# Unread matmuls ahead of the first spectra, u as the moving operand of the gate sums, and unsummed pairs of Q rows, in a gated mix of two long convolutions

## The chip, the cores and the metric

The kernel runs on one core of one Trainium2 chip. Its time is the device time in microseconds (us), the median of several runs. TensorE is called PE in what follows, its weight loads PEld, VectorE DVE, ScalarE ACT, GpSimd POOL, and the queue that starts most transfers SP.

## The reference

All inputs are bf16. The sequence has 2048 steps, the width is 448, and there are 256 complex modes for every channel. The two branches are long causal convolutions over the sequence, mixed by a gate that is computed from the same input x.

```
g = sigmoid(sum over channels of x * gate_w)              # one value for each step

# branch A: a state-space layer
K[d, l] = Re sum_n C[d,n] * exp(dt[d] * A[d,n] * l) * dt[d] * B[d,n]      # l = 0 .. 2047
a = causal_conv(x, K) + x * Dskip

# branch B: a gated convolution with a given kernel
kv = (k convolved with 4 taps of shift_k) * v
b = x * (causal_conv(kv, ssm_k) + kv * ssm_D)

out = g * a + (1 - g) * b
```

The reference computes the convolutions with transforms of length 4096.

## The kernel before

**Stages.** The 448 channels are cut into four groups of 112 (a group of 32 partitions each), and these into NQG = 4 quarters H of NC = 28. A convolution goes through a transform that is factored into matmuls. `spread` multiplies every column with a small matrix (Wc, or WcK for the kernel K) into the PSUM tile ps_c, which ACT casts to a spectrum tile zs (zsK for the kernel's). `transform` then multiplies it with W2 (s_W in the profile), four groups of eight matmuls of 112 columns, each through a PSUM tile ps and an ACT cast back to zs. `swapped` makes a copy zsS of a spectrum with its halves exchanged, by two transfers on SP. `products` multiplies spectra on DVE. `stage_a` (matrix R, the tile sa_R; PSUM tile ps_a; ACT casts into U) and `stage_b` (matrix G, the tile sb_G; PSUM tile ps_b) are the way back. Every quarter of each branch takes these stages. The spectra of branch B come from raw rows of ssm_k (skraw) and from kv, those of branch A from x (the tile uu) and from K.

**The kernel K.** K is made in NBLK = 8 blocks of 14 columns in `KGen.block`, so that 2048 steps arise from a product of two smaller tables of powers. DVE builds a table TQ (kg_TQ, NQ = 21 rows) and a table TP (kg_TP, 32 rows) of complex powers by doubling. `mult` makes the four real products of some rows with the power of one exponent (into P4, kg_P in the profile), and `add` sums pairs of them to new rows. Row groups of TQ arise for the exponents 4, 2, 256, 1 and 512. The rows for exponent 1 are not used for any further power. Then 224 small matmuls, `lhsT=TQ[:, :, c, m]` and 32 moving columns of TP, sum over the modes in the PSUM tile pk, in four column groups of the array (`tile_position=(0, 32 * g)`). ACT casts pk to kg_S, and `gather` sums the right rows of it with a table of zeros and ones (ga_sel), which `Consts.rows` and `Consts.gather` have set up at the start, into kg_KT.

The powers of one exponent, exp and sine for each mode, are made for two blocks at a time in `Tables.levels` (tiles ks_mag, ks_ph, ET): DVE makes phases, ACT the exponentials and sines. The two functions lie in different tables of ACT, and a change from one to the other costs a table load.

**The gate sums.** x * gate_w is summed over channels on PE. For every l of 112, a matmul has `uu[:, :, l]` (128 partitions, 64 columns that lie 112 elements apart) as weights and `gwt[:, l, :]` (32 columns) as the moving operand, and all 112 add up in one PSUM tile, ps_gate:

```
for l in range(112):
    nc.tensor.matmul(pg[0:64, 0:32], lhsT=uu[:, :, l], rhs=gwt[:, l, :], start=(l == 0), stop=(l == 111))
```

A copy (gx) and a transpose spread the sums over the partitions, and tanh gives the gate (gt, and from it gb and og).

**The start.** k arrives in sixteen transfers. `kvt` products on DVE, matmuls with an identity (PSUM tile ps_v) and ACT casts convolve it with the four taps. Meanwhile the modes are transposed (ps_m), and the matrices W2, G, R and so on are made of phases on DVE and sines on ACT.

**The end.** The last spectrum, K of the last quarter, is transformed in two halves by `transform_half`; `stage_a_half` and `stage_b` follow, then `epilogue_A` and the stores of the result.

**The order.** Nothing is issued when the code calls it. `Order` records all the calls of all engines (6452 here) in a list, and `Order.issue` issues them in the order of the string ORDER, a list of call numbers that was written beforehand; each engine runs its own instructions strictly in that order. This is why nearly all instructions have line 146, the line of `issue`, in the profile. They are told apart by their tiles.

Of the kernel before, what the change touches and what calls it, by code (L numbers as in the profile page):

```python
# [31 lines left out]
NQ = 21  # L32
# [9 lines left out]
    "600 25 576 30 164 1 190 525 24 36 188 196 162 189 175 177 23 34 186 191-192 187 176 193 526 534 26 31 552 173 "  # L42
    "171 580 174 536 581 0 32 160 593 537 2 166 172 528 33 73 535 598 21 179 17 35 540 11 10 14 3 22 28 75 16 6 182 "
    "178 13 18 12 29 15 7 19 198 184 9 38 591 8 5 20 4 37 181 74 65 180 183 39 76 201 27 161 550 197 577 168 200 167 "
    "41 542 163 544 589 169 165 194 79 590 40 582 170 541 195 42 599 583 52 199 185 202 586 592 69 584 587 585 588 "
    "100 46-47 203 50 72 51 553 44 595 204 594 551 43 538 48 45 110 66 49 557 68 77 101-108 90 53 78 55 554 71 56 539 "
    "150 54 596 63 556 111-118 67 109 62 597 70 527 91-98 555 80 61 64 119 529 140 531 151-158 99 530 234-241 602 545 "
    "130 141-148 159 242 215-222 543 532 120 149 225-232 548 205-212 223 233 213 267 214 549 243-250 224 252-259 547 "
    "251 81-88 533 546 260 121-128 89 319-326 129 262 268-283 261 327 131-138 284 264 263 285-300 139 266 302-317 265 "
    "301 575 516 499 318 493 1104 366 574 469 346-353 486 365 1106 1103 354 367 1105 471 502 470 364 474 473 472 468 "  # L50
    "481 370-385 490 573 477 570 498 562 578 507 567 489 513 561 482 560 494 815-830 483 512 478 579 479 495 484 487 "
    "491 496 488 480 492 485 503 603-616 521 497 522 504 1121 524 523 500 508 505 514 1108 617-630 501 509 517 1110 "
    "506 1109 631-644 510 518 1111 511 645-658 1119 558 1112 1122 1113 659-672 568 1117 673-686 572 559 1115 475 2483 "
    "687-700 566 515 563 1118 571 565 701-714 1124 831 1120 386 60 57-58 1126 798-813 1114 59 715 476 421-428 564 "
    "1123 716 814 1116 1107 1125 429 1510-1517 1846 717 1127 569 1476-1491 1518 2514 328-335 2498 1492 2515 781-796 "
    "519 1847 2497 2489 1848 718 404-419 2488 1129 520 720 1131 2487 719 1128 2491 2486 2492 2485 1133 797 1130 1132 "
    "420 1459-1474 1136 601 336 772-779 1135 1475 337-344 2490 1134 387-402 345 1137 2484 1849 832-839 780 1138 403 "
    "355-362 1850 840 1331-1362 1851 363 1267-1330 2499 1852 369 430-437 448-455 439-446 1853 368 1139-1202 1854 456 "
    "2518 2500 447 2519 1857 1203-1266 1856 2516 1855 438 946-953 2517 2509 1363 1860 1859 2510 1862 2511 1858 "
    "457-464 2520 755-770 2512 954 2521 1382-1421 2506 2502 465 1864 1493-1508 2505 2503 1422 1844 467 937-944 2507 "  # L60
    "1364-1380 1842 2504 1843 1381 1841 1509 1432-1439 2508 2538 2513 2494 721-736 2537 771 2493 2539 466 2495 "
    "738-753 737 754 2496 1639-1646 2533 2532 2540 2501 858-873 2558 2529 945 2528 2557 1861 1845 2522 901-908 2559 "
    "874 1863 1865 909 928-935 1867 1869 1647 2560 892-899 1871 936 2561 910-917 1866 900 919-926 918 1870 955-962 "
    "927 841-856 1868 2530 1872 1455 1648-1655 963 2563 1456 857 875-890 2531 2523 2565 1656 964-971 2524 2568 891 "
    "1873 1440 1038-1101 1874 2534 2525 1875 972 1441-1446 2535 1876 2552 1457 2069-2100 1877-1940 2544 2553-2554 "
    "2546 2005-2068 2549 1102 2545 2555 2550 1941-2004 2536 1458 2548 1447 2543 2541 2556 2551 3326 2547 1448-1453 "
    "2526 1613-1628 2542 2570-2571 2101 3328 3963 3327 2527 2573 1666-1673 1454 2562 1629 1657-1664 1423-1430 1674 "
    "2575 1579-1594 2564 1665 2566 1519-1534 2567 1595 3329 973-1036 3999 3966 3990 3965 3989 3970 3998 3330 3968 "
    "2569 3967 2197-2212 3972 1037 3964 1431 3971 2120-2159 2572 2213 1570-1577 6189 2160 1596-1611 1578 3331 1535 "
    "2102-2118 2574 1536-1551 3969 3333 2119 2577 1612 1630-1637 2186-2191 1552 2576 1553-1568 2579 1638 2578 "  # L70
    "2995-3002 1569 2585 2214-2229 3003 2193-2194 3332 2248-2255 2230-2246 2584 2256 1684-1691 3991 1711-1774 3334 "
    "2586 3335 2247 2581 1692-1700 3974 3973 2583 2192 2944-2959 1701 1775 2170-2178 1702-1709 2580 2960 2587 "
    "2161-2168 1675-1682 1710 3992 2961-2976 3336 1683 2582 3338 2716-2779 2977 3337 2196 2652-2715 2169 3975-3976 "
    "3985-3986 2195 2179-2184 3987 2588-2651 2185 2780-2811 3994 2812 2257-2272 3339 3995 3340 3996 3988 3342 3993 "
    "3978 4000 3344 3977 2317-2324 3350 2273 2335-2342 2813-2829 3979 4001 2308-2315 3983 2830 3352 2325 2831-2870 "
    "3341 4003 2316 3343 2915-2922 4004 2343 3345 2326-2333 3997 2871 1776-1839 3347 2334 3982 3349 3346 4005 2923 "
    "4013 3055-3062 4006 4002 2890-2895 1840 2291-2306 4007 3063 3351 6192 3984 2978-2993 3021-3036 2307 4018 4017 "
    "2994 2274-2289 4012 4019 3348 3037 3980 2924-2931 3353 3981 2344-2351 2290 3354 2352 3728-3735 3355 4029 4020 "
    "2904 2906-2913 3356 2905 4038 3549-3580 4037 4028 4008 4032 4039 4048 4026 3421-3484 4040 4021 4033 4009 4023 "
    "4041 3357-3420 4030 4042 4010 4044 3736 4046 3485-3548 2914 4047 4011 4014 4049 2418-2481 2932 4050-4051 4807 "  # L80
    "4806 4025 4053 4808 4055 4052 4022 4015 4031 2353-2416 4054 4016 2482 4036 4034 4027 4057 4024 3677-3692 3581 "
    "2896 2417 4035 5383 2933-2940 3693 4059 2897-2902 3038-3053 6195 2941 3711-3726 4065 2903 3054 3694-3709 2943 "
    "3727 2872-2879 5388 5392 5384 5393 5387 5406 2942 5386 5389 2880 5385 2881-2888 5391 5390 3710 5405 3115-3122 "
    "5394 4043 2889 3806-3813 5395 4809 3098-3113 4045 4810 4064 3600-3639 3123 3814-3822 5396 4066 3114 3081-3096 "
    "5418 4811 3640 3824-3831 3823 4056 3582-3598 4813 3097 3004-3019 4058 5419 3599 4060 3124-3131 4061 3832 "
    "3650-3657 3132 4062 3064-3079 4063 3658 4817 4067 3142-3149 5407 3666-3671 3080 4815 4132-4195 3672 5415 4816 "
    "3150 3641-3648 5414 4196-4259 4818 3649 5408 5416 4821 3020 5398 4823 5397 4825 5399 3659-3664 4260-4291 5417 "
    "3665 4068-4131 5400 4827 5401 5403 5402 4404-4411 4292 4820 4819 4822 5404 3169-3176 4412 4812 5420 4395-4402 "
    "4824 4293-4309 3177 4814 3151-3158 4826 4310 3133-3140 3159 4311-4350 4830 3141 3160-3167 5421 4351 4832 3673 "
    "3196-3259 3168 5428 5438 3674 5429 4403 5437 4828 5430 3178-3185 5439-5440 4377-4382 3260 4834 4475-4482 "  # L90
    "3186-3194 5458 5409 5424 5449 4833 3261-3324 4829 4835 5451 5455 4831 4836 5452 5456 5454 3195 5431 5029-5060 "
    "5423 5410 4965-5028 5444 3676 5442 5448 5443 3797-3804 3325 4901-4964 5453 6190 5447 5446 5445 5441 3675 5450 "
    "4727-4742 3805 5422 4837-4900 4384 4483 6191 5425 4458-4473 4385 5468 5844-5846 5471 5061 5457 5426 5411 "
    "3788-3795 5470 5459 4474 5473 5460 3796 3754-3769 5412 4383 5461 5413 5432-5433 4352-4359 5475 5427 5462 3770 "
    "4413-4421 5466 4386-4393 5464 4360 3737-3752 4394 5467 5847 4370-4375 5434 3771-3786 4423 3753 4376 4744-4759 "
    "3787 4422 4361-4368 4743 4710-4725 4760 3833-3896 5848 4726 5469 5435 5472 4369 4424-4439 3897 5463 4441-4456 "
    "4440 5474 5465 5062-5078 4535-4542 5436 5476 5079 4518-4533 5481 4543 4457 5080-5119 5478 4484-4499 5483 4534 "
    "5477 4544-4551 5120 4501-4516 4500 5479 5485 5121-5128 4552 4761-4768 4517 5484 3898-3961 4769 5480 5486 5129 "
# [60 lines left out]
class Consts:  # L159
# [31 lines left out]
    def onehot(self, name, n, col, scale=1.0, pool=None):  # L191
        t = (pool or self.pool).tile([P, n], f32, name=name)
        self.nc.vector.tensor_scalar(out=t[:], in0=self.iota(name + "_j", [[1, n]]), scalar1=col[:, 0:1],
                                     scalar2=scale, op0=ALU.is_equal, op1=ALU.mult)
        return t
# [788 lines left out]
```

## Time and profile before

| what | value |
|---|---|
| median of 3 runs | 301.66 us (301.40 to 303.37) |
| the profiled execution, its own time | 302.91 us |
| its span, from first to last instruction | 300.7 us |
| mean granted TensorE clock | 0.861 |
| busy: PE, PEld | 224.0 us, 197.8 us |
| busy: DVE, ACT, POOL | 268.4 us, 257.7 us, 9.7 us |
| matmuls | 5386 |
| ACT table loads | 15, of 1283 ns each |

The busy time of an engine counts its compute instructions. Matmuls overlap each other and their ends are modelled, so PE's busy time says that matmuls were under way and not that the array was full. In the rows of forty slices each digit is the busy share of a slice (7.5 us) in tenths, 9 being 90% or more; in the row PEclk it is the granted clock. A row of groups names the line, the engine, the operation and the tiles written and read, with the shapes and the count; then come the busy time in us and the mean of one in ns, and behind the second bar the idle time of the engine ahead of them, with what ended it. A line of the timeline begins with the start and the length in us.

### The profile page before, as it was taken

To read this page: it belongs to the slowest core of one execution; us is meant where nothing else is said; L and a number is where in the kernel's file an instruction comes from. 1 tells how busy PE (TensorE), PEld (TensorE's weight loads), DVE (VectorE), ACT (ScalarE), POOL (GpSimd) and SP (SyncE) were. 2 spreads that over 40 slices of the span, in tenths; PEclk is the share of its full clock that TensorE was granted. 3 is DMA by queue.
4 is the path that set the end of the run, shared out by engine and by line. 5 is a ranking of instruction groups with operands and counts; after the bars stand their busy time and mean duration, and the time that the engine had idled before them with its cause. 6 is when DMAs were issued, how large, how long until landed. Compare 5 with 4: busy or idle time off the path is not lost.

```text
span 300.7 us, 12051 instructions
## 1 busy us (share of the span) xinstructions
PE 224.0 (74%) x5386; PEld 197.8 (66%) x5386; DVE 268.4 (89%) x536; ACT 257.7 (86%) x413; POOL 9.7 (3%) x42
## 2 busy tenths in 40 slices
PE   0186664997956867998887696978869999869740
PEld 0033444996954766997777685867759988769730
DVE  8999999987987989899999999989999999983850
ACT  4899989979979999899799999999999999906600
POOL 6003000010000000000000000000000000000000
PEclk9999795557689797997999777999788999969995
DMA  6999999210234051040001410005050000900058
GB/s 126 185 216 168 175 154 282 43 23 0 49 80 63 0 125 50 2 104 25 5 2 34 95 49 2 2 5 121 7 124 2 2 4 20 220 17 4 3 112 134
DMA packets 53380, 21.34 MB, mean 71 GB/s; under 512 B 48720, under 2 KB 51664, under 8 KB 53328
## 3 DMA queue, kind: packets, MB, share of 16 engines
q1 hardware_dynamic: 48768, 19.42, 34.6%
q10 hardware_dynamic: 4560, 1.15, 2.0%
q8 instruction: 42, 0.69, 1.0%
q14 instruction: 10, 0.08, 0.1%
HBM read 10.01 MB, written 3.21 MB: 44 GB/s over the span
## 4 chain that ended last, share of the span: by engine, by line
ACT 34%; DVE 16%; PE 9%; issue 3%; DMA 2%; DVEq 0%; ACTq 0%; SPq 0%
ACT zs L146 13%; ACT ET L146 6%; ACT U L146 5%; ACT zsK L146 5%; DVE kg_P L146 4%; PE ps_a L146 3%; DVE kg_TP L146 3%; DMA zsS<-zs 2%; DVE zs L146 2%; ACT L146 2%; DVE ug L146 2%; DVE zsS L146 2%; PE ps_b L146 1%; PE ps_c L146 1%; PE pk L146 1%
## 5 line engine op out<-in xcount | busy, mean ns | idle before, releaser
L146 ACT CAST zs<-ps 128x896 bf16<-128x896 f32 x48 | 43.5, 935 | 1.2 <-PE ps L146 1.2
L146 DVE TENSOR_TENSOR kg_P<-kg_TQ,ET 128x896 bf16<-128x896 bf16 (+2 forms) x64 | 43.9, 705 | 0.6 <-ACT ET L146 0.4
L146 ACT CAST zs<-ps_c 128x1024 bf16<-128x1024 f32 (+1 forms) x48 | 42.4, 925 | 0.8 <-PE ps_c L146 0.8
L146 PEld LDWEIGHTS <-s_W 128*128 128x128 bf16 x544 | 32.7, 107 | 14.7 <-issue 12.2
L146 PE MATMUL ps_a<-sa_R,zs 128*128 128x128 bf16 x224 | 35.6, 245 | 5.0 <-ACT zs L146 3.6
L146 PE MATMUL ps<-zs,s_W 128*128 128x112 bf16 x384 | 30.0, 233 | 9.3 <-ACT zs L146 7.9
L146 PE MATMUL pk<-kg_TP,kg_TQ 128*21 128x32 bf16 x1792 | 30.9, 238 | 7.7 <-issue 5.1
L146 PE MATMUL ps_a<-sa_R,zsS 128*128 128x128 bf16 x224 | 34.9, 243 | 0.7 <-DVE zsS L146 0.7
L146 PEld LDWEIGHTS <-zsS 128*128 128x128 bf16 x224 | 30.8, 154 | 5.7 <-issue 4.2
L146 PEld LDWEIGHTS <-kg_TQ 128*21 128x21 bf16 x1792 | 27.8, 121 | 9.9 <-issue 8.3
L146 PE MATMUL ps_b<-U,sb_G 128*128 128x28 bf16 x1024 | 28.3, 176 | 6.1 <-ACT U L146 2.5
L146 DVE TENSOR_TENSOR kg_P<-kg_TP,ET 128x1792 bf16<-128x1792 bf16 (+1 forms) x32 | 30.7, 968 | 1.8 <-ACT ET L146 1.8
L146 PEld LDWEIGHTS <-sb_G 128*128 128x128 bf16 x1024 | 27.6, 97 | 7.1 <-issue 5.6
L146 PEld LDWEIGHTS <-zs 128*128 128x128 bf16 x224 | 30.7, 153 | 2.4 <-DVE zs L146 0.8
L146 ACT CAST U<-ps_a 128x1024 bf16<-128x1024 f32 (+2 forms) x30 | 28.3, 947 | 3.3 <-PE ps_a L146 3.2
L146 PEld LDWEIGHTS <-uu 128*64 128x64 bf16 x336 | 28.1, 212 | 3.4 <-DMA skraw<-in_B_ssm_k_dram 2.2
L146 DVE TENSOR_TENSOR kg_TQ<-kg_P 128x896 bf16<-128x896 bf16 (+2 forms) x64 | 27.3, 441 | 0.1
L146 ACT ACTIVATE ET<-ks_ph 128x448 bf16<-128x448 int16 x40 | 22.8, 595 | 1.6 <-DVE ks_ph L146 1.6
L146 PEld LDWEIGHTS <-scratch 128*128 128x128 bf16 x65 | 7.2, 112 | 25.0 <-DVE oA_f L146 10.8
L146 ACT ACT_TABLE_LOAD x15 | 19.2, 1283 | 4.3 <-DMA kt<-in_B_k_dram 4.0
L146 ACT CAST zsK<-ps_c 128x512 bf16<-128x512 f32 (+2 forms) x27 | 20.9, 779 | 0.7 <-PE ps_c L146 0.7
L146 DVE TENSOR_TENSOR kg_TP<-kg_P 128x896 bf16<-128x896 bf16 (+2 forms) x40 | 19.8, 500 | 0.0
(132 smaller groups left out, 455.5 us busy)
## 6 DMA issues: line engine op xcount, KB each, us to landing
zsS<-zs SPq DMA_DIRECT2D x16, 448.0 KB, 4.3
kt<-in_B_k_dram SPq DMA_DIRECT2D x16, 112.0 KB, 4.1
skraw<-in_B_ssm_k_dram SPq DMA_DIRECT2D x16, 112.0 KB, 4.4
vt<-in_B_v_dram SPq DMA_DIRECT2D x4, 448.0 KB, 7.1
uu<-in_A_u_dram SPq DMA_DIRECT2D x4, 448.0 KB, 5.9
xfd<-ks_hold SPq DMA_DIRECT2D x2, 672.0 KB, 6.2
ks_xf<-xfd SPq DMA_DIRECT2D x3, 336.0 KB, 2.9
out_dram<-ug SPq DMA_DIRECT2D x8, 112.0 KB, 4.7
```

The source lines that it names most:

```text
L146: ins = f(*args, **kw)
```

## The change

Three pieces of the computation change, some small tiles move, and ORDER is a new list throughout.

1. 640 matmuls are added that write columns 448 to 512 of the PSUM tile pk, which nothing reads. They have R[:, 0:128] as weights and 64 columns of R as the moving operand. The code makes 20 times 32 calls. In the new ORDER they lie in 40 groups of 16, from the first instruction of PE on to shortly ahead of the gate's last matmul.
2. In the gate sums the operands change places: gwt[:, l, :] (32 columns) is the weight and uu[:, :, l] (64 columns) moves. The matmuls go to the four column groups in turn, so that four partial sums arise on 128 partitions. A matmul with a table of zeros and ones (gx[:, 64:192]) sums the four and spreads the result over the partitions; it takes the place of the transpose.
3. For exponent 1, `leaf` writes the two products of which each component is the sum as two rows of TQ, without adding them. TQ has 25 rows (NQ = 25): 17 to 24 are the pairs, and the other rows get new numbers. As the kernel matmuls are linear in the rows, the sum of a pair is taken later, in `gather`: both rows of a pair get the same index in the table of zeros and ones (q_half and the minimum).
4. The index columns and masks of `field`, `onehot` and `stage_c` and the tile dj lie in the scratch tile and not in tiles of their own, and ept shares its buffer with kg_KT.

```diff
-NQ = 21
+NQ = 25
...
-    "600 25 576 30 164 1 190 525 24 36 188 196 162 189 175 177 23 34 186 191-192 187 176 193 526 534 26 31 552 173 "
...
+    "604 25 177 27 23 28 24 29 1 166 198 525 26 32 175 162 196 176 171 160 173 0 37 172 1246 192 174 197 2 161 178 "
...
     def field(self, name, shift, mask, mult=1.0, add=0.0, pool=None):
...
-        ti = self.pool.tile([P, 1], i32, name=name + "_i")
+        ti = self.carve(1)
...
-        tf = (pool or self.pool).tile([P, 1], f32, name=name + "_f")
+        tf = self.carve(1).bitcast(f32)
...
+        def named(q):
+            return q if q < 4 else q + 13 if q < 8 else q - 4
+
         def q_of(grp, r):
-            return first[grp] + {1: (0, 4, 2, 6, 1, 5, 3, 7), 2: (0, 4, 2, 6), 4: (0, 4), 8: (0,)}[step[grp]].index(r)
+            return named(first[grp] + {1: (0, 4, 2, 6, 1, 5, 3, 7), 2: (0, 4, 2, 6), 4: (0, 4), 8: (0,)}[step[grp]].index(r))
...
+        def leaf(dst, src, e):
+            r, m = EQ[:, entry_of(e) + 1], src.shape[1]
+            for c in range(2):
+                V.tensor_tensor(out=TQ[:, dst + c:dst + c + 2 * m - 1:2], in0=src[:, :, c].unsqueeze(2).to_broadcast([P, m, 2, M]),
+                                in1=bass.AP(r.tensor, r.offset + c * M, [list(r.ap[0]), [0, m], [-M, 2], [1, M]]), op=ALU.mult)
+
...
         q256 = mult([TQ[:, 0:4]], 256)
-        q1 = mult([TQ[:, 0:4]], 1)
-        add(TQ, 8, q256)
-        add(TQ, 4, q1)
-        q512 = mult([TQ[:, 0:2], TQ[:, 8:10]], 512)
+        leaf(17, TQ[:, 0:4], 1)
+        add(TQ, 4, q256)
+        q512 = mult([TQ[:, 0:2], TQ[:, 4:6]], 512)
...
-    cons.gather(cons.field("q1", 0, 31), maskg)
+    q_col, q_half = cons.field("q1", 0, 31), cons.carve(1)
+    V.tensor_scalar(out=q_half, in0=cons.pidx[:], scalar1=31, scalar2=None, op0=ALU.bitwise_and)
+    V.tensor_scalar(out=q_half, in0=q_half, scalar1=17.0, scalar2=None, op0=ALU.add)
+    V.tensor_scalar(out=q_half, in0=q_half, scalar1=1, scalar2=None, op0=ALU.logical_shift_right)
+    V.tensor_tensor(out=q_col[:], in0=q_col[:], in1=q_half, op=ALU.min)
+    cons.gather(q_col, maskg)
...
+    for _ in range(20):
+        for i in range(32):
+            nc.tensor.matmul(pk[:, 448:512], lhsT=R[:, 0:128], rhs=R[:, 128:192], start=True, stop=True)
...
-            t = kgp.tile([P, 32, NC], bf16, name="ept")[:, 0:n]
+            t = kgp.tile([P, 32, NC], bf16, name="ept", tag="kg_KT")[:, 0:n]
...
-    V.tensor_copy(gx[:, 0:64], ident[:, 0:64])
+    V.tensor_scalar(out=gx[:, 64:192], in0=cons.iota("four_j", [[0, 4], [1, 32]]), scalar1=a1[:, 0:1], scalar2=None, op0=ALU.is_equal)
     pg = psum.tile([P, 512], f32, name="ps_gate", tag="ps")
     for l in range(112):
-        nc.tensor.matmul(pg[0:64, 0:32], lhsT=uu[:, :, l], rhs=gwt[:, l, :], start=(l == 0), stop=(l == 111))
-    nc.scalar.copy(gx[0:64, 64:192].rearrange("p (g a) -> p g a", g=4), pg[0:64, 0:32].unsqueeze(1).to_broadcast([64, 4, 32]))
-    nc.tensor.transpose(out=pg[:, 128:192], in_=gx[0:64, 64:192], identity=gx[0:64, 0:64])
+        q = 32 * (l % 4)
+        nc.tensor.matmul(pg[q:q + 32, 0:64], lhsT=gwt[:, l, :], rhs=uu[:, :, l], start=(l < 4), stop=(l >= 108), tile_position=(0, q))
+    nc.scalar.copy(gx[:, 0:64], pg[:, 0:64])
+    nc.tensor.matmul(pg[:, 128:192], lhsT=gx[:, 64:192], rhs=gx[:, 0:64], start=True, stop=True)
```

## The prediction

> **What bounds the kernel now.** I read the busy table and the forty slices first, then the stretches of 7.5 us, the groups with shapes kept apart, the timeline of 40 to 115 us, the waits, the chain, and the end.
>
> ```profile
> PE   0186664997956867998887696978869999869740
> ...
> DVE  8999999987987989899999999989999999983850
> ACT  4899989979979999899799999999999999906600
> ...
> PEclk9999795557689797997999777999788999969995
> ```
>
> DVE and ACT are nearly full in every slice up to the 35th; PE is not. Up to 262.5 us the stretches sum to 248.3 us for DVE and 247.3 for ACT, 94 to 95% of each. So there is no single bound: two engines run full side by side, each holds the other up, and the span falls only as far as both lose work or waits. The clock row has one long low place, slices 7 to 12, and there both full engines have their holes:
>
> ```profile
> 52.50:60.00 7.50, 7.50 (x66) 7.50 (x66) 7.37 (x24) 7.47 (x18) 0.24 (x1) 0.50 0.26 41
> 60.00:67.50 7.50, 7.19 (x75) 7.01 (x76) 6.62 (x16) 5.47 (x13) 1.30 (x1) 0.50 0.17 26
> 67.50:75.00 7.50, 5.61 (x89) 4.83 (x86) 5.68 (x14) 7.23 (x17) 0.00 (x0) 0.73 0.00 0
> ...
> 82.50:90.00 7.50, 4.44 (x156) 3.80 (x146) 6.13 (x19) 5.34 (x10) 0.00 (x0) 0.83 0.34 81
> 90.00:97.50 7.50, 4.52 (x95) 3.56 (x92) 6.06 (x15) 6.93 (x12) 0.46 (x1) 0.94 0.41 63
> ```
>
> After start and length the columns are PE, PEld, DVE, ACT, POOL, clock. From 60 to 97.5 us (75 to 82.5, not shown, is full) DVE stands 5.5 us and ACT 5.1. PE is without a gap at 52.5 to 60, at half clock: it is doing the gate sums, with the first spectra queued behind them.
>
> ```profile
> 51.66 13.03 PEld L146 LDWEIGHTS <-uu 128*64 128x64 bf16 x110 [2.17 <-DMA skraw<-in_B_ssm_k_dram]
> 51.69 13.11 PE L146 MATMUL ps_gate<-gwt,uu 128*64 128x32 bf16 x110 [2.01 <-ACT ET L146]
> ```
>
> A gate matmul takes 13.11/110 = 119 ns, and it is its weight load that takes them.
>
> **Gate sums, u moving.** Before, 64 columns of u, 224 bytes apart, are the weights. The Trainium skill, "SBUF — State Buffer", in its note on SBUF "cachelines" (16 bytes), says that each access to a new line pays. The row agrees: 119/64 = 1.86 ns a column. That rule speaks against the change, since u is just as strided as the moving operand, and by it a gate matmul would still cost 119 ns. The nearest row for a strided moving operand in four column groups is the kernel matmul:
>
> ```profile
> 81.58 2.10 PE L146 MATMUL pk<-kg_TP,kg_TQ 128*21 128x32 bf16 x128
> ```
>
> It takes 16.4 ns each, so a round of four takes 66 ns, or 2.0 ns for each of its 32 moving columns 448 bytes apart. The price per column is there, but four groups pay it at once. A round of four gate matmuls then takes 64 x 2.0 = 131 ns: 28 rounds are 3.7 us in place of 13.3, which is 9.6 us less on PE. If the groups do not overlap it is 13.3 again: a gain of 0. I take 9.6, by the row. The ACT copy becomes 128x64 for 64x128, the transpose a matmul, the DVE copy (0.35 us) a comparison of like size: nothing.
>
> **The 640 unread matmuls.** Each loads 128 contiguous columns and moves 64. Near rows:
>
> ```profile
> 43.96 0.55 PE L146 MATMUL ps<-zs,s_W 128*128 128x112 bf16 x8 [1.81 <-ACT zs L146]
> ...
> 68.70 0.93 PE L146 MATMUL ps<-zs,s_W 128*128 128x112 bf16 x8
> ```
>
> Without the last one's latency (0.21 and 0.28 us), that is 49 ns apiece for 112 columns at clock 1.0 and 93 at 0.5. By columns, with 2 to 3 ns of overhead, 64 take 30 ns at full clock and 53 at half: 19 to 34 us in all. In PE's new order 512 of them stand ahead of the gate sums and 128 among and after them (runs of 32, 32, 80, 16, 16, 16, 64, 256; then 16, 32, 80). They wait for nothing but sa_R, but PE is in order, so transposes, spreads and transforms queue behind them. Before, PE was idle about 13 us between 13.2 and 51.7 us. At 30 ns, 512 take 15.4: the gate sums start 2 us later, end at 51.7 + 2 + 3.7, and the other 128 add 3.8: 61 us, 3.5 us ahead of the old 64.7. Above 30 + 3.5/640, some 36 ns a matmul, the work behind comes later than before.
>
> What they should buy is the clock. "TensorE: Matmul & The Clock Gate", Part 1, says that PE reaches full clock after one busy window of about 3.4 us. By that rule the 13 us of unbroken gate sums would have brought it; the row shows 0.50 throughout. What is counted is evidently not the page's busy: a gate matmul moved only 32 columns in 119 ns. Unread matmuls move 64 without a break, and unbroken 448-column matmuls from 14.1 us did reach full speed (373 ns each at first, 189 from 19.2 us). So I expect full clock from 17 to 20 us and, the trap of the gate sums gone, through most of the first 75. Behind the gate sums each group of eight 112-column matmuls then takes 0.35 us less. The strided spreads of kv gain nothing: a pair takes 120 ns at either clock.
>
> Of the 5.5 and 5.1 us of holes I give back 4.0. The rest are DVE's waits for an ET from ACT (1.27 and 1.23 us in 67.5 to 75), which a faster PE does not touch. Ends: 0 and 7, the latter with holes of the next 15 us that descend from these.
>
> **Unsummed pairs.** Per block, one product over four rows and its sum give way to two products of 128x896 (16 in the new DVE list):
>
> ```profile
> L146 DVE TENSOR_TENSOR kg_P<-kg_TQ,ET 128x896 bf16<-128x896 bf16 x40 | 24.2, 618 | 0.1
> ...
> L146 DVE TENSOR_TENSOR kg_P<-kg_TQ,ET 128x1792 bf16<-128x1792 bf16 x16 | 17.3, 1084 | 0.5 <-ACT ET L146 0.4
> ...
> L146 DVE TENSOR_TENSOR kg_TQ<-kg_P 128x896 bf16<-128x896 bf16 x24 | 14.6, 616 | 0.0
> ```
>
> 8 x (1084 + 616 - 2 x 618) = 3.7 us less on DVE. No row writes every other row of TQ, so 618 is bounded above by the slow rate of the same size (ug<-ps_b,uu: 1083), which turns the gain into a loss of 3.7. The inner runs stay 112 contiguous elements, as in rows that run at 618, so I take 618. TQ grows from 21 to 25 rows: a kernel matmul of 1792 costs between 0 more and 25/21 of 16.4, 3 ns, which is 0.7 us a block. Only the last block's lies bare; I take 0.3 there. The extra ones in the gather table add no instruction, the four extra index operations are 0.06 us each, and the small tiles moved into scratch cost nothing but what room they free.
>
> **The order.** All five lists are new. ACT's table loads fall from 15 to 13:
>
> ```profile
> L146 ACT ACT_TABLE_LOAD x15 | 19.2, 1283 | 4.3 <-DMA kt<-in_B_k_dram 4.0
> ```
>
> That is 2.6 us off ACT, certain by the list. On SP, other loads now stand among the sixteen of kt: the last is issued 21st instead of 16th, 5 x 0.67 = 3.4 us later. DVE has three other kvt products (2 us each) and two ks_hold products to do first, so I cost it at nothing; without that cover, 1 to 3 us. POOL's list moves only small iotas.
>
> In the tail, the half-0 transforms of the last spectrum (32 matmuls of 56 columns and four ACT casts of 0.53 us) and their products move behind the last kernel matmuls. That frees ACT ahead of them and fills its holes after:
>
> ```profile
> 267.84 0.53 ACT L146 CAST kg_S<-pk 128x448 bf16<-128x448 f32 x1 [5.43 <-PE pk L146]
> ```
>
> But both halves of the last stage-a (56 matmuls at 65 to 72 ns) now follow 128 ps_b matmuls (25 ns each), so PE ends its queue some 0.8 us later than now. The chain has a hole inside those last 224 kernel matmuls, 2.45 us of "issue" at 263.97, just as an instruction block is fetched behind a zsS transfer; I leave it as it is (2.5 either way). Tail with the wider TQ: +1.0.
>
> **Sum.** DVE -3.7 and ACT -2.6 alternate as the later one: -3.0. Holes -4.0. Tail +1.0. Together -6.0 us. From the profiled execution (302.9; its span 300.7) that is 296.9; it ran 1.25 above the median of the three runs, 301.66, so the runs should give 295.7.
>
> **Rivals.** About 1% (3.0 us) is what a measurement of this kernel tells from no change.
>
> - *The holes were not PE's.* They may hang on ET and on the zsS swap (1.3 us of waits), or the gate groups do not overlap, so that the matmuls save only what the fillers spend. Left are -3.0, +1.0 and little else: 299.7, no change. For it: several waits in 67 to 97 us name ACT ET. Against: the longest hole, ACT's 1.8 us at 65, is named after ps_gate. Chance 0.14.
> - *The fillers hold PE at half clock.* One mechanism, at 16 to 75 us: at 53 ns, 512 take 27 us against 13 of idle time, and the gate starts 14 us later; with the other 128 the spectra come at 76 us against 64.7, 11 us late. ACT has some 11 us of exponentials and sines that need no PE, about 4 of them still uncommitted; it then waits about 7 us more. 301.7 - 3.0 + 1.0 + 7 = 306.7. It decides above 36 ns a matmul. For it: every matmul before 19.2 us ran at half clock, and 80 KB of added instructions are fetched while DMA is full (share over 1.0 to 52 us). Against: dense matmuls did raise the clock. Chance 0.08.
> - *All holes close.* The middle idles 11.9 us on DVE and 9.3 on ACT after 60 us; 7 back, and the tail no longer: 301.7 - 3.3 - 7 = 291.4. For it: DVE and ACT wait mostly for each other, so one freed wait frees others. Against: all the lists are new, and new waits come with them. Chance 0.18.
>
> **The numbers.** Forecast 295.7, chance 0.60. The range runs from 290.0 (all holes, and a little in the tail) to 300.5 (no holes, or the pairs at half gain). Faster by over 1% (below 298.6): 0.60 + 0.18 = 0.78. Within 1%: 0.14. Slower by over 1%: 0.08.
>
> **What would show it.** Right: ps_gate in under 5 us of PE, starting near 52; PEclk full from slice 3 through slice 9; fillers near 30 ns; two rows of 896 at about 618 x16 in place of the product and the sum; 13 table loads; DVE busy 264 to 265 us, ACT about 255; holes in 60 to 97 us of 2 us instead of 5. Wrong: fillers at 45 ns or more, PE without a gap until 65 us with ACT waiting for it; gate matmuls near 119 ns; pair products over 900 ns; or DVE and ACT as full as before with new holes further on.

## The result, and the profile after

The changed kernel takes **298.67 us** (median of four runs, 298.48 to 298.73) beside 302.12 of the kernel before on the same chip (301.40 to 303.37): a ratio of 0.988, with a 95% interval of 0.9844 to 0.9917. That is 3.45 us by the medians, and 4.3 us between the two profiled executions (298.65 with a span of 296.3; before 302.91 and 300.7). The forecast was 6.0 us.

The busy slices of the page after:

```profile
PE   0298989886967869979999698779579969869740
...
DVE  7999999899999999997999899999999997936850
ACT  4999799999999999999999999989998957728500
...
PEclk9999999989795997978999799899768997979955
```

The clock row is what the unread matmuls were to bring: it is full up to slice 8 and reads 8 tenths in slice 9, where slices 7 to 9 read 5 before. DVE and ACT are still the two full engines. The four stretches that had the holes, in the columns of before (start, length, PE, PEld, DVE, ACT, POOL, clock):

```profile
60.00:67.50 7.50, 6.73 (x106) 6.05 (x102) 7.29 (x18) 7.47 (x15) 0.00 (x0) 0.78 0.01 2
67.50:75.00 7.50, 5.14 (x95) 4.84 (x93) 7.50 (x15) 7.50 (x15) 0.00 (x0) 0.96 0.00 1
...
82.50:90.00 7.50, 4.51 (x107) 3.68 (x104) 7.29 (x22) 7.50 (x12) 0.00 (x0) 0.87 0.42 63
90.00:97.50 7.50, 6.26 (x116) 5.50 (x116) 7.50 (x17) 7.24 (x13) 0.40 (x1) 0.68 0.01 2
```

In these four DVE stands 0.4 us in place of 5.5 and ACT 0.3 in place of 5.0. The holes are gone. The groups, with shapes kept apart (busy us, mean ns of one | idle before, and what ended it); the first row is the kernel before, the others the changed one:

```profile
L146 PE MATMUL pk<-kg_TP,kg_TQ 128*21 128x32 bf16 x1792 | 30.9, 238 | 7.7 <-issue 5.1 <-DVE kg_TP L146 2.6
...
L151 PE MATMUL pk<-kg_TP,kg_TQ 128*25 128x32 bf16 x1792 | 31.4, 239 | 13.5 <-issue 11.5 <-DVE kg_TP L151 1.6 <-DVE kg_TQ L151 0.3
...
L151 PE MATMUL pk<-sa_R 128*128 128x64 bf16 x640 | 22.2, 197 | 14.6 <-DVE sa_R L151 13.3 <-issue 1.3
...
L151 ACT ACT_TABLE_LOAD x13 | 16.7, 1283 | 4.1 <-DMA kt<-in_B_k_dram 3.9
...
L151 DVE TENSOR_TENSOR kg_TQ<-kg_TQ,ET 128x896 bf16<-128x896 bf16 x16 | 9.7, 623 | 0.2
L151 DVE TENSOR_TENSOR kg_P<-kg_TQ,ET 128x1792 bf16<-128x1792 bf16 x8 | 8.7, 1086 | 0.0
...
L151 PE MATMUL ps_gate<-uu,gwt 128*32 128x64 bf16 x112 | 3.9, 299 | 0.0
```

The gate sums take 3.9 us for 13.3, the unread matmuls 22.2 us in all, the new half products 623 ns each, and there are 13 table loads. DVE is busy 264.7 us (before 268.4), ACT 254.0 (257.7). The first two rows hold what was not foreseen: the kernel matmuls stood 5.1 us for "issue" (idle time for which the profile shows no wait) before, and 11.5 now. In the chain of waits, read between 236 and 262 us, two such pieces lie on the path:

```profile
239.25 2.52 PE pk L151 x147
241.77 2.65 issue
...
256.22 2.87 PE pk L151 x153
259.09 2.72 issue
```

The one at 259 stood at 264 before (2.45 us); the one at 241.8 is new. Earlier on the same chain lie two more, 2.72 us at 163.4 and 1.30 at 194.3.

**What these stops are.** TensorE's instructions are fetched in blocks of 16 KB, and the trace has each fetch, on a queue of its own. These are the rows of that queue before and after (fetches, MB, share of the DMA engines):

```profile
q8 instruction: 42, 0.69, 1.0%
...
q8 instruction: 47, 0.77, 1.1%
```

42 fetches for 5386 matmuls and 47 for 6027 are one for every 128 matmuls with their weight loads. Counted from the first matmul, most fetches that nothing disturbs begin between the 87th and the 125th of a block; the stops lie at about the 87th of the next one, where the fetch that was due in the block before has not landed yet. The stop at 241.5 shows it: the swap transfer (zsS, two of 448 KB) sets out at 239.62, the fetch begins 2.4 us later, at 241.98, and lands at 242.86, and TensorE goes on at 244.42. From 160 us on there are five stops over 1 us, of 2.95, 1.54, 1.51, 2.89 and 2.96 us, 11.9 in all. (They are counted from the start of the last matmul to the start of the next, some 0.24 us more than the chain has.)

So I set two theories against each other. **F** (for fetch): these stops are where the missing part of the gain went. **W** (for waits): it went to new dependency waits of the new lists. Two more were at stake: whether the unread matmuls or the short gate sums had closed the holes, and what the rows were worth.

### The profile page after: what moved, and what is told of

Its sections match the earlier page's. It is cut to its first block, busy times and chain, and to the rows that moved or that the text cites. A ratio compares the mean times of both kernels' runs of the same rounds, so it can differ in the third digit from the quotient of the medians.

```text
span 296.3 us, 13325 instructions
## 1 busy us (share of the span) xinstructions
PE 230.1 (78%) x6027; PEld 206.0 (70%) x6027; DVE 264.7 (89%) x540; ACT 254.0 (86%) x411; POOL 7.5 (3%) x43
## 4 chain that ended last, share of the span: by engine, by line
ACT 46%; PE 20%; DVE 12%; SPq 7%; issue 6%; DMA 5%; DVEq 0%; ACTq 0%
ACT zs L151 17%; ACT ET L151 11%; SPq L151 7%; PE pk L151 5%; PE ps_a L151 5%; ACT zsK L151 4%; ACT U L151 4%; ACT L151 4%; PE ps L151 4%; DVE kg_P L151 3%; ACT ks_mag L151 3%; DMA kt<-in_B_k_dram 3%; DVE kg_TP L151 3%; PE ps_b L151 3%; DMA vt<-in_B_v_dram 2%
## 5 line engine op out<-in xcount | busy, mean ns | idle before, releaser
L151 ACT CAST zs<-ps 128x896 bf16<-128x896 f32 x48 | 44.5, 955 | 0.6 <-PE ps L151 0.6
L151 ACT CAST zs<-ps_c 128x1024 bf16<-128x1024 f32 (+1 forms) x48 | 43.8, 941 | 0.2 <-PE ps_c L151 0.2
L151 PE MATMUL pk<-kg_TP,kg_TQ 128*25 128x32 bf16 x1792 | 31.4, 239 | 13.5 <-issue 11.5
L151 PEld LDWEIGHTS <-kg_TQ 128*25 128x25 bf16 x1792 | 28.2, 127 | 16.4 <-issue 14.6
L151 DVE TENSOR_TENSOR kg_P<-kg_TQ,ET 128x896 bf16<-128x896 bf16 (+2 forms) x56 | 36.1, 655 | 0.1
L151 PE MATMUL ps_a<-sa_R,zs 128*128 128x128 bf16 x224 | 34.1, 240 | 1.0 <-ACT zs L151 0.6
L151 PE MATMUL pk<-sa_R 128*128 128x64 bf16 x640 | 22.2, 197 | 14.6 <-DVE sa_R L151 13.3
L151 PE MATMUL ps_a<-sa_R,zsS 128*128 128x128 bf16 x224 | 33.4, 237 | 0.1
L151 PEld LDWEIGHTS <-sa_R 128*128 128x128 bf16 x640 | 21.1, 101 | 15.7 <-DVE sa_R L151 13.3
L151 DVE TENSOR_TENSOR kg_TQ<-kg_P 128x448 bf16<-128x448 bf16 (+2 forms) x56 | 23.4, 423 | 0.2
```

The lines of the kernel that those rows point to most:

```text
L151: ins = f(*args, **kw)
```

## The experiments

"The ratio" is always to the kernel before, run on the same chip in the same session. Its medians in the five sessions are 302.1 to 303.0 us, so a difference of medians across sessions is rough to that extent. All twelve experiments, below the changed kernel:

| kernel | median us | ratio, 95% interval |
|---|---|---|
| changed kernel | 298.67 | 0.988, 0.9844 to 0.9917 |
| 688 unread matmuls | 297.90 | 0.9864, 0.9804 to 0.9925 |
| 664 | 297.94 | 0.9855, 0.9801 to 0.9910 |
| 560 | 296.56 | 0.9826, 0.9766 to 0.9886 |
| none | 297.93 | 0.9848, 0.9793 to 0.9904 |
| none but 52 + 20 placed ones | 296.08 | 0.9787, 0.9763 to 0.9810 |
| old gate sums | 308.92 | 1.0212, 1.0186 to 1.0238 |
| old gate sums, no unread | 302.78 | 1.0017, 0.9999 to 1.0035 |
| old rows | 300.15 | 0.9917, 0.9890 to 0.9945 |
| swap in four parts | 294.14 | 0.9745, 0.9702 to 0.9788 |
| swap in four parts, no unread | 293.98 | 0.9734, 0.9700 to 0.9769 |
| kernel before, new gate sums | 298.82 | 0.9901, 0.9871 to 0.9930 |
| kernel before, swap in four parts | 299.15 | 0.9877, 0.9852 to 0.9901 |

### The place of the stops: 688, 664 and 560 unread matmuls

```
 for n in the calls of the order:
-    issue call n
+    issue call n twice if 1197 <= n < 1245     # 688 (664: from 1221 on)
+    leave call n out if 1165 <= n < 1245       # 560
```

> The changed kernel with 48 more unread matmuls (688), the last 48 issued twice. What the traces of the two kernels show: TensorE's instructions come in 16 KB blocks, one per 128 matmuls with their weight loads; block k is fetched as TensorE passes about matmul 128k+97, and where it has not landed TensorE stops at about 128k+215. In the changed kernel all five stops in the kernel matmuls (2.95 us at 163.1, 1.54 at 194.0, 1.51 at 214.2, 2.89 at 241.5, 2.96 at 258.9) are at such a place with a swap transfer (zsS) moving between the two places. Theory F (the missing part of the gain is in these stops): 48 more matmuls move every block border 48 matmuls, 1.5 us, earlier in the kernel matmuls, so that the fetches are asked for ahead of the transfers; moving the borders against the trace of the changed kernel makes the five stops some 4 us in all in place of 11.9, the one near 241 under 1 us and the one near 259 about 1.2. Time 2 to 4 us below the changed kernel (295 to 296.7), although there is more work. Theory W (the gain went to new dependency waits of the new order): 48 matmuls more change nothing or cost up to 1.4 us: 298.4 to 300.

> The changed kernel with 24 more unread matmuls (664): half the step of 688, to the side of the borders that is as bad as the changed kernel's. Theory F: borders 0.75 us earlier, still inside the transfers; stops of about 11 to 12 us in all, the one near 241 about 3 us; time within 0.7 us of the changed kernel (298 to 299.4), so that 24 and 48 more differ by 2 us or more. Theory W: 664 and 688 differ by no more than the 24 matmuls, 0.7 us.

> The changed kernel with the last 80 of the unread matmuls left out (560). Block borders as with 688, because 688 - 560 is one block of 128 matmuls. Theory F: the same stops and the same time as with 688 within 1 us (295 to 297), unless the 80 fewer let the clock fall around the gate sums, which the granted clock between 50 and 75 us would show. Theory W: the time of the changed kernel, 298 to 299.5.

The stops moved as forecast, the time did not. With 664 they are at 163.1 (3.37 us), 194.4 (2.37), 215.1 (1.08) and 257.4 (3.89); the one near 241 has moved to 245.2 (1.84), into the gather. With 688 and with 560 the stop at 163 is gone and so is the one inside the kernel matmuls near 241. The chain between 234 and 262 us with 688 runs through DVE, with no stop of TensorE, up to 254, and has one left:

```profile
238.32 0.19 DVE kg_TQ L153
...
242.35 0.54 DVE kg_P L153
...
254.47 2.13 PE pk L153 x117
256.60 2.29 issue
```

But the medians of 688 and 664 are the same, where F had asked for 2 us. The trace tells in part why: a border moved out of the kernel matmuls stops TensorE a little later, in the transforms behind them. With 688 there are 2.30 us at 243.2 (ps<-zsK). The stop near 194 grew from 1.54 to 2.61 us, and the one at 256 kept 2.5 where I had 1.2: with 0.99 at 167.1 these are 8.4 us, where I had forecast some 4. Single runs of all three lie between 296.1 and 299.0, and the profiled ones, 296.7 and 296.1 with the two good places against 298.8 with the bad one, are not enough for a verdict. The place of a stop can be steered; what that is worth these three do not show.

### No unread matmuls

```
+    leave call n out if 605 <= n < 1245
```

> The changed kernel with all 640 unread matmuls left out; 640 matmuls are five blocks exactly, so the block borders in all that follows stay where they are in the changed kernel. Theory C (the unread matmuls keep the clock up, and that closes the holes): granted clock 0.50 from about 20 to 75 us; the 112 gate matmuls take up to twice as long (4 to 7.5 us); DVE idle in 60 to 97.5 us back from 0.9 to 2.5 us or more, and 1.5 to 3.5 us more time (300 to 302). Rival (the shorter gate sums alone close the holes, the clock does not matter): within 0.5 us of the changed kernel. Theory F asks here only that the stops near 163, 241 and 259 are still there, each 2.4 us or more.

The rival (the short gate sums alone close the holes) holds: 297.93, no slower than with them (the intervals overlap). These are its stretches:

```profile
45.00:60.00 15.00, 7.10 (x152) 6.02 (x152) 14.00 (x45) 14.97 (x38) 0.79 (x2) 0.61 0.91 190
60.00:67.50 7.50, 5.57 (x64) 4.91 (x64) 7.29 (x18) 7.47 (x15) 0.00 (x0) 0.50 0.01 2
67.50:75.00 7.50, 5.24 (x95) 4.96 (x93) 7.50 (x15) 7.50 (x15) 0.00 (x0) 0.94 0.00 1
```

The clock is back at 0.61 and 0.50, and the holes stay shut: DVE 7.29 and 7.50, to the digit as with the unread matmuls. From 45 to 60 us DVE even works 14.00 us for 13.10 in the changed kernel. And the stops are still there, 2.74 us at 162.3, 3.07 at 239.2, 2.45 at 257.0, as five whole blocks less should have it.

### The gate sums: old in the new kernel, new in the old

```
-        q = 32 * (l % 4)
-        nc.tensor.matmul(pg[q:q + 32, 0:64], lhsT=gwt[:, l, :], rhs=uu[:, :, l], ..., tile_position=(0, q))
+        nc.tensor.matmul(pg[0:64, 0:32], lhsT=uu[:, :, l], rhs=gwt[:, l, :], ...)
```

The copies and the transpose behind the sums go back with them.

> The changed kernel with the gate sums of before (u as the weights, 112 matmuls; the number of TensorE's instructions and the block borders stay). The kernel without unread matmuls has shown that these do not close the holes of 60 to 97.5 us: DVE idles 1.0 us there at a granted clock of 0.61 to 0.85. Theory G (the short gate sums close them): the sums take about 13 us again, also at full clock, because the row of before was the weight load's; DVE idle in 60 to 97.5 us back from 0.9 to 3 us or more, time 2.5 to 5 us above the changed kernel (301.2 to 303.7). Rival O (the new order closes them): less than 1 us of idle time and of time more. Rival C2 (the old sums at full clock take half): about 7 us of sums and up to 1.5 us of time.

> The changed kernel with the gate sums of before and none of the 640 unread matmuls: the fourth corner of the square. Theory G: as with the old sums and the unread matmuls within 1 us, since these are worth nothing either way (301 to 303.5). Rival C (a full clock helps where TensorE is late): 1.5 us or more above the kernel with old sums and unread matmuls, so that the unread matmuls help only where the gate is long. Rival O: within 1 us of the kernel with new sums and no unread matmuls (297.9).

Theory G (the short gate sums close the holes) is right, and with unread matmuls the effect is larger than forecast. Without unread matmuls the old sums cost 4.85 us (302.78 against 297.93); with them 10 (308.92 against 298.67). The unread matmuls make a difference only beside the old sums, and there they cost 6.1 us. These are the groups and the stretches of the old sums with unread matmuls:

```profile
L151 PE MATMUL ps_gate<-gwt,uu 128*64 128x32 bf16 x112 | 13.7, 274 | 0.0
```

```profile
60.00:67.50 7.50, 7.50 (x72) 7.26 (x72) 2.42 (x7) 3.90 (x8) 0.00 (x0) 0.50 0.00 0
67.50:75.00 7.50, 7.38 (x156) 7.18 (x155) 5.16 (x11) 5.51 (x11) 0.00 (x0) 0.88 0.02 4
```

TensorE is full, DVE works 2.42 of 7.5 us. In this one kernel a gate matmul of the old form takes 118.2 ns at the clock of 0.50 and 118.5 at 1.0; one of the new form 27.4 (no unread matmuls) and 27.5 (with them). Neither follows the clock, so a full clock could not help either. Rivals C (a full clock helps where TensorE is late) and C2 (the old sums at full clock take half) fall.

The kernel before with nothing new but the gate sums:

> The kernel before, in its own order, with the gate sums of the change alone (u moving, the 4x32 sum matrix made from an iota at hand). In the changed kernel without unread matmuls the gate sums were worth 4.85 us (302.78 to 297.93). If they are worth that in any order (Theory G): 297 to 298.5, the holes of 60 to 97.5 us down from 5.5 to under 2 on DVE, and all that the rest of the change brings nets to about nothing. If the new order is a part of it (the old one was laid out around sums of 13 us): 299.5 to 301.5, with DVE holes of 2 to 4 us left in 60 to 97.5.

298.82, 3.65 us below the kernel before (3.0 by the ratio) and within 0.2% of the whole change. Both halves of the expectation are half right: in its stretches the hole of 60 to 75 us is closed, that of 84 to 97.5 only in part. The third row is the kernel before:

```profile
60.00:75.00 15.00, 10.17 (x137) 9.23 (x138) 14.52 (x34) 14.73 (x33) 0.71 (x1) 0.58 0.07 9
...
84.00:97.50 13.50, 10.71 (x183) 9.10 (x183) 11.74 (x31) 11.79 (x18) 0.39 (x1) 0.61 0.23 37
...
84.00:97.50 13.50, 7.46 (x163) 5.97 (x161) 10.69 (x29) 10.77 (x18) 0.46 (x1) 0.87 0.30 53
```

In the kernel before DVE reads 12.30 and 10.69 in these two. (The profiled execution of this run, 300.3 us, never had more than 0.85 of the clock.) So what I had taken for one hole was two, with two causes. The second is named below.

### The rows of exponent 1, summed again

```
-        leaf(17, TQ[:, 0:4], 1)
+        add(TQ, 17, mult([TQ[:, 0:4]], 1))     # 21 rows; the gather table sums nothing
```

> The changed kernel with the rows of exponent 1 summed as before: one product of 1084 ns and one sum of 616 in place of two half products of 618, 21 rows in place of 25 in the kernel matmuls, everything else and all orders kept. Theory P (the prediction's step: DVE work on the path): eight times 0.46 us, DVE busy 3.7 us more, time 2 to 3.7 us above the changed kernel (300.7 to 302.4). Rival A (ACT's turns and TensorE's stops hide DVE's part): below 1.5 us more. Rival W25 (25 rows slow the kernel matmuls): the mean of a kernel matmul falls from 31.4 ns with 21 rows; if 30.5 or more, no.

300.15, a ratio of 0.9917 for 0.988: 0.37% of 302.5, **1.1 us** (1.5 by the medians), though DVE is busy 268.2 us, 3.5 more. The two intervals overlap, so that anything from nothing to 2.5 us is possible. Rival A (other engines hide DVE's part) fits best: two thirds of DVE's saving is not on the path. The 25 rows are nearly free: all kernel matmuls together take 31.0 us with 21 rows and 31.4 with 25 (us, where the expectation has ns).

### One mark in each run: 52 and 20 placed matmuls

```
+    leave call n out if 657 <= n < 1245
+    issue call 605 another 20 times after the last kernel matmul of the block before the last
```

> The changed kernel with only the first 52 of the 640 unread matmuls, and 20 more put behind the kernel matmuls of the last block but one. What the five traces with stops have in common: TensorE asks for its next block of instructions at every 128th matmul (number 86 of a block) and stands still at the next such mark if it has not come; a run of 224 kernel matmuls stops when two marks lie inside it and a swap transfer is moving. In the kernel without unread matmuls the first marks of the last five runs are at their matmuls 42, 31, 24, 29 and 48, so that a second one falls 128 later into each. 52 matmuls more move them to 118, 107, 100, 105, and the 20 more move the last to 104: one mark in each run. Theory F: no stop over 1 us in the last five runs (12.7 us over 1 us in the kernel without unread matmuls, from 100 us on); time 2 to 3 us below that kernel's (297.93), 295 to 296, the most of it between 239 us and the last kernel matmul. Theory W: 297.5 to 298.5. A third outcome, stops gone and time kept, would say that they are covered.

296.08: 1.85 us under the kernel without unread matmuls, a little less than F asked (the intervals just overlap). None of the last five runs of kernel matmuls has a stop over 1 us, but the chain (234 to 262 us) shows two of them where they went:

```profile
239.83 1.21 PE pk L154 x46
241.04 3.16 issue
...
258.23 0.66 PE ps_a L154 x8
258.89 1.47 issue
```

The first waits among the 20 placed matmuls, the second in stage a. These stops were not saved by steering; they moved to where, by the time, less hung on them.

### The transfer beside the stops: the swap in four parts

```
     for r in range(2):
-        nc.sync.dma_start(swap[64 * r:64 * r + 64], zs[64 - 64 * r:128 - 64 * r])
+        for k in range(0, 32, 8):
+            nc.sync.dma_start(swap[64 * r:64 * r + 64, k:k + 8], zs[64 - 64 * r:128 - 64 * r, k:k + 8])
```

> The changed kernel with each swap transfer (448 KB) issued as four of 112 KB, nothing else. If TensorE's instruction fetch waits behind the transfer that is in flight (Theory F; in the stops the fetch began 2.4 or 4.4 us after the swap's start, that is after one or both of its two transfers of about 2.2 us each), smaller transfers let it in sooner: fetch within 1 us of the mark, the five stops from 160 us on down from 11.9 us in all to under 6, and 1 to 2.5 us off the time (296.2 to 297.7). If the fetch is late for another reason (a fixed delay of TensorE's own at these places, or plain bandwidth shared by both), the stops and the time stay (298.2 to 299.5).

> The changed kernel without the 640 unread matmuls and with the swap transfers in four parts each: gate sums, rows and order of the change alone. Theory F: the gain of the split on top of the 297.93 without unread matmuls, 295.5 to 297. If the split does nothing: 297.5 to 298.5.

294.14 and 293.98: **4.5 us off the changed kernel** (4.1 by the ratios), more than expected, by an edit that touches no arithmetic. The five stops from 160 us on have become three, of 1.66, 1.56 and 1.21 us. The kernel matmuls' row and the chain from 234 to 262 us, both with unread matmuls:

```profile
L157 PE MATMUL pk<-kg_TP,kg_TQ 128*25 128x32 bf16 x1792 | 31.5, 239 | 8.7 <-issue 6.1 <-DVE kg_TP L157 2.2 <-DVE kg_TQ L157 0.3
```

```profile
240.03 1.33 issue
...
250.26 1.96 DMA zsS<-zs
...
256.08 0.98 issue
```

"Issue" falls from 11.5 to 6.1 us, on the chain from 2.65 and 2.72 to 1.33 and 0.98. The fetch waits behind the transfer in flight: with a smaller one it comes sooner. That of the stop at 240.0 now begins at 238.50, 1.5 us ahead of the stop, where in the changed kernel it began after TensorE had stopped. That the swap would only land earlier does not explain the gain, since in the changed kernel neither a DVE wait nor the chain names it, and now it stands on the chain itself.

> The kernel before, whole, with each swap transfer in four parts. A control for the split of the changed kernel (298.67 to 294.14), which also lets each part start as soon as its quarter of the source is ready. Theory F (the split is worth the stops that it takes away): the kernel before has two stops over 1 us in its kernel matmuls in place of five (1.84 us at 114.1, 2.68 at 263.7), so it gains 0.5 to 2 us (300.5 to 302). If the split helps by an earlier swap, whatever TensorE's instructions do, it gains as much as in the changed kernel: 3.5 to 5 us (297.5 to 299).

The control went against F: 299.15, **3.8 us** off, nearly as much as in the changed kernel. I had counted stops in the kernel matmuls only. A third one of the kernel before lies just behind them, in a transform (and a fourth, 1.3 us at 169.8, in stage b). Here are TensorE's instructions of 82 to 90 us in the kernel before (start, length, ..., idle before it):

```profile
83.61 0.57 PE L146 MATMUL ps<-zs,s_W 128*128 128x112 bf16 x8
87.24 0.77 PE L146 MATMUL ps<-zs,s_W 128*128 128x112 bf16 x8 [3.06 <-ACT zs L146]
```

and with the swap in parts:

```profile
83.66 0.57 PE L152 MATMUL ps<-zs,s_W 128*128 128x112 bf16 x8
85.05 0.55 PE L152 MATMUL ps<-zs,s_W 128*128 128x112 bf16 x8 [0.82 <-ACT kg_S L152]
```

The profile puts the 3.06 us down to ACT's zs, a cast that starts at 85.95. But with the swap in parts the same eight matmuls start at 85.05, ahead of the same cast (85.76): they do not need it. A fetch ran from 84.84 to 85.92, behind the swap of 81.06 to 85.25, and TensorE went on 1.3 us after it landed; in the five stops of the changed kernel it was 1.3 to 1.6. The stretches of the kernel before in four parts:

```profile
82.50:90.00 7.50, 5.51 (x205) 4.56 (x194) 7.44 (x20) 7.50 (x13) 0.00 (x0) 1.00 0.38 72
90.00:97.50 7.50, 5.67 (x68) 4.88 (x68) 7.36 (x21) 6.89 (x11) 1.56 (x1) 0.58 0.21 30
```

DVE reads 7.44 and 7.36 for 6.13 and 6.06. By the next kernel matmuls, which begin at 108.1 us in place of 111.0, 2.9 us are there. The earlier landing of the swap that follows (104 to 112 us) is hardly a part of it: DVE waits 1.3 us for it before and 1.1 with the parts, and DVE's lead is there already at the first product behind the hole, before and with the parts:

```profile
97.57 0.39 DVE L146 TENSOR_TENSOR kg_P<-ET 128x448 bf16<-128x448 bf16 x1 [0.72 <-ACT ET L146]
...
94.34 0.39 DVE L152 TENSOR_TENSOR kg_P<-ET 128x448 bf16<-128x448 bf16 x1
```

## Why the prediction was right, and where it was not

The direction was right; the size was overstated, 6.0 us against 3.45. Step by step:

- **Gate sums: right.** 3.7 us foretold, 3.9 measured, the fourfold overlap as the kernel matmul's row had it. The Trainium skill's rule on strided access ("SBUF — State Buffer", SBUF "cachelines") spoke against it. The price per column stayed, 110 ns for a round of 64 strided columns, 1.7 ns each, where the weights had 118 (1.8 each); but four matmuls share a round, 27.5 ns each.
- **Unread matmuls: the mechanism right, the value wrong.** 53 ns before 17 us and 29 to 31 after, the clock at 1.0 from 16.3 us on for 47.8 us: all as foretold. But "what they should buy is the clock" was the step that failed. The clock bought nothing, since the holes shut as well without it. The old gate sums, which were late, ran at 118 ns at either clock, as the prediction itself noted for the spreads of kv (a pair takes 120). The skill's page "TensorE: Matmul & The Clock Gate", Part 1, says that sustained matmuls bring the full clock; for the unread ones the trace agrees (1.0 from 16.3 us, 3 us after the first at 13.3), for the old gate sums it does not (0.50 throughout).
- **Holes -4.0: right in size, wrong in cause.** The gate sums alone bring 3.65 us in the old order and 4.85 in the new. Of the 5.5 us of holes the first half (60 to 75 us) was the gate's. The second, at 84 to 97.5, hung in the kernel before mostly on an instruction fetch, which the prediction did not name: the new sums alone took 1.1 of its 2.8 us on DVE, the swap in parts alone 2.6. Why it shut in the changed kernel is not shown: no stop lies there, but with 688 a stop of 1.4 us is back at 82.4, and DVE still idles only 1.1 us from 60 to 97.5. That the sum of both came out near 4.0 is luck. The first rival, the holes not being TensorE's at all, falls; of the named cause of the second rival, unread matmuls that hold TensorE up, 6.1 us are real, but only beside the old sums.
- **Work -3.0: the term that was mis-sized.** DVE's 3.7 us and ACT's (3.7 less busy, 2.6 of it table loads) arrived in the busy table. On the path the rows are worth 1.1 (at most 2.5). The error was to take most of the work of a 95% full engine as time. That the other two thirds became idle time because ACT's turns and TensorE's stops set the pace as well is argued, not shown. The table loads were not tried by themselves.
- **Tail +1.0:** from the last kg_S to DVE's last instruction 23.7 us for 23.0: +0.7.
- **The fetch hole, left "as it is (2.5 either way)":** that one stayed, 2.72 us on the chain. That the same thing would come a second time, at 241.8, was not foreseen, though the hole and the fetch behind a swap were both in the prediction's text.
- **The third rival, all holes closed (291.4),** had the holes nearly right and the time wrong: those of 60 to 97.5 us shut, and others opened, at 241.8 and at 45 to 60, where DVE stands 1.9 us with the unread matmuls and 1.0 without. (Its sum takes 3.3 us for the work, where the forecast takes 3.0.)

With the measured sizes the sum is -1.1 (rows) -3.65 (gate) +0.7 (tail) = -4.05, or -3.4 with the gate sums by the ratio; measured are 3.45 by the medians and 4.3 profiled. The tail's part lies in the new order, and the unread matmuls' (0 to +0.7) is within the scatter. F as the *whole* answer falls. The swap in parts is worth some 4 us to either kernel, so the stops cancel: with it on both sides the change brings 0.9745/0.9877, 1.3%, hardly more than its 1.2% without. What remains of F, argued from the chain and the control, is that the new stop at 241.8 (2.65 us) took back about what the old one at 84 had cost (2.9).

W was not tested by an edit, but DVE's idle time says where the rest went. It is 32.3 us in all before and 31.6 after, so the 4.4 us of the span are nearly all less work (3.7); this is a count on one engine and names no cause. The idle time moved. From 60 to 130 us it fell from 8.1 to 1.8; but it rose from 2.2 to 4.2 before 60 us, from 2.0 to 4.1 between 130 and 200, and from 1.8 to 4.0 between 200 and the end of the last kg_S. With the swap in parts the changed kernel has 2.5 and 0.4 in the last two, so there it was mostly the stops. The time before 60 us lies ahead of the five stops and stays unexplained. The rest of the change without gate sums and unread matmuls stands at a ratio of 1.0017, so the rows' 1.1 us, and whatever the saved table loads are worth, are lost again in the new lists, stops and tail included; how much to each stays open.

## What to carry to other kernels

A hole on full engines can have two causes lying side by side: undo each part alone before crediting one, and doubt the engine that a wait names when another run starts the same work ahead of it. Before raising the clock for a stretch, see from two rows at different clocks whether its instructions follow the clock at all. In a kernel with thousands of small matmuls, count them in blocks of 128 (one fetch of 16 KB here), look for "issue" once in each block, and try large transfers beside them in parts: here that was worth more than the whole change, and the changed kernel with the swap in four parts is the best of the study, with the unread matmuls (294.14) or without (293.98, 0.9734).

## What the runs showed of the hardware

- In the traces of all fourteen kernels TensorE's stops of over 0.8 us that the profile puts down to "issue" lie near one place of its blocks of 128 matmuls, the 87th to 95th by the trace's count (78th to 89th with the swap in parts). In the changed kernel's five it went on 1.3 to 1.6 us after the late fetch had landed, not at once. A fetch takes 0.9 to 1.8 us. In the changed kernel those of the five stops began 2.4, 4.2, 5.7, 2.4 and 4.6 us after the swap ahead of them (two transfers of 448 KB) had set out.
- A matmul whose 64 weight columns lie 224 bytes apart takes 118 ns at half and at full clock (old gate sums in the changed kernel). A matmul that moves 64 such columns in four column groups takes 27.4 at 0.50 (no unread matmuls) and 27.5 at 1.0 (with them).
- 13 us of unbroken gate sums left the clock at 0.50 (kernel before). Of the unread matmuls, which move 64 columns each, 52 ran at 53 ns before it rose to 1.0, and none so slowly after (changed kernel).
